# Value rows in groups of 64 columns, a 512 + 128 split of the last output tile, and its last store on ScalarE's queue

## The chip, the cores and the metric

The kernel runs on one core of one Trainium2 chip. Its engines are TensorE (PE in the profile; PEld is its weight load), VectorE (DVE), ScalarE (ACT), GpSimd (POOL) and SyncE (SP). Each has its own instruction queue and they meet through semaphores. DMA transfers are issued here from SyncE and ScalarE. The metric is the device time of one execution in microseconds (us), lower is better; three executions of the kernel before gave 269.50, 269.57 and 269.68, median 269.57.

## The reference

One layer norm feeds two branches whose results are added to the input: linear attention with a learned feature map (32 heads of 20 columns), and a gated MLP. S = 2048 rows, D = 640, F = 1536, all in bf16.

```python
xn = layernorm(x)
q, k, v = split(xn @ wqkv)                       # 32 heads, 20 columns each
pq, pk = q @ w_phi, k @ w_phi                    # per head
phi = lambda p: concat(softmax(p), softmax(-p))  # 40 features
kv  = einsum("bhsf,bhsd->bhfd", phi(pk), v)      # summed over all rows
z   = einsum("bhsf->bhf", phi(pk))
o   = (phi(pq) @ kv) / (phi(pq) . z + 1e-6)
h   = silu(xn @ w1) * (xn @ w3)
out = x + o @ wo + h @ w2
```

## The kernel before

The 2048 rows are T = 16 tiles of 128 rows. w_phi is folded into the query and key weights (Wqp, Wkp) on TensorE, so one product gives the features. Each piece of work is a generator in a list of streams (L768 to L910). A planner (L915 to L956) builds the next step of each stream, sums costs written into the source for every engine, and commits the step that can start first; ties go by the list. So the order on every engine follows from these costs, and an edit that changes a cost or a dependency can move steps. `_Program` finds dependencies by memory: an operation's accesses are cut into granules of GRAN bytes (L67 to L95), and two operations that touch one granule are ordered (L120 to L152). PSUM counts by whole banks. The source line of all instructions but DMAs is therefore L102, and of DMAs L114; the profile tells them apart by tiles.

What the change touches, in order of time:

- **Warm-up** (`warm_up`, `idle`, L506 to L513): TensorE multiplies zeros into PSUM bank 7 while the first rows of x load, 7 times 512 columns and 11 times 128.
- **Norms** (`ln_half`, `ln_rstd`, L453 to L471): statistics in `bst`, mean and variance in `mv`, scale in `rstd`, a row of each for every tile (L290 to L292).
- **Values** (`v_part`, `v_tile`, `v_store`, L556 to L566): 10 matmuls of 320 columns put a tile's values into two PSUM banks, columns 0 to 319 of each. ScalarE copies them to `v2`, where a head takes 21 columns, 20 values and a one. The ones are written once by a GpSimd memset (L450), between the norms.
- **Keys** (`k_tile`, `k_norm`, L568 to L582): ScalarE writes exp of both signs to `ekt`; VectorE sums it, and GpSimd scales it in two halves of 640 columns a tile.
- **Key-value sum** (`kv_sum`, L590 to L596): for every tile 11 matmuls, one for each group of three heads (the last has two). The weights are 128 columns of `ekt` from column 120·g, the moving operand is `v2` from column 21·h, 63 columns wide (42 in the last group). It runs in four parts of four tiles (L837 to L854). `kv_store` masks the sum and puts it to `KVc`, in groups of 64 columns; its unused columns are cleared by a memset on GpSimd.
- **Query product** (`q_tok`, L660 to L672): 11 matmuls of 63 columns a tile, weights `eqT`, moving operand `KVc` from column 64·g. They write the same PSUM columns as the sum (`at_group`).
- **Output** (`out_tile`, L693 to L712): 17 weight tiles (5 of oT, 12 of hT) by 640 columns in two halves of 320, one add of the input on VectorE, one store. The last tile is done in 384 and then 256 columns, each with its own add and store from SyncE.

`v2` shares its memory with `oT`; the arena of 212,832 bytes for a partition is full.

Of the kernel before, what the change touches and what calls it, by code (L numbers as in the profile page):

```python
# [3 lines left out]
ACT = mybir.ActivationFunctionType  # L4
# [5 lines left out]
D = 640  # L10
H = 32
DH = 20
F = 1536
T = S // 128
DC = D // 128
FC = F // 128
NB = S // 512
NG = 11
# [1 line left out]
DEN_EPS = 1e-6  # L20

ENGINES = ("PE", "ACT", "DVE", "POOL", "SP")
GRAN = 32


def heads_of_chunk(c):
# [17 lines left out]
class _Program:  # L44
# [22 lines left out]
    def regions(self, ap):  # L67
# [25 lines left out]
        for r in runs:  # L93
            g.update(range((b + r * esz) // GRAN, (b + (r + length) * esz - 1) // GRAN + 1))
        return list(g)  # L95
# [154 lines left out]
def bass_parallel_sum__linear_kernel_hedgehog__glu_gated_swiglu__prompt_kernel(  # L250
# [11 lines left out]
    bf = DT.bfloat16  # L262
    LAG = 4.0
    QLEAD = 2
    IDLE1, IDLE2 = 11, 8
    f32 = DT.float32
    P = _Program(nc)

# [5 lines left out]
    def region(size):  # L274
        o = top[0]
        top[0] = o + (size + 31) // 32 * 32
        assert top[0] <= arena_size, top[0]
        return a0 + o

    def new(name, shape, dtype, offset=None):  # L280
        size = mybir.dt.size(dtype)
        for n in shape[1:]:
            size *= n
        return P.sbuf(name, shape, dtype, region(size) if offset is None else offset)
# [2 lines left out]
    GM = new("GM", [128, DC, H], bf)  # L287
    phi_s = new("phi_s", [128, DC, DH], bf)
    BDc = new("BDc", [128, DC, 8 * DH], bf)
    bst = new("bst", [128, T, 16], f32)  # L290
    mv = new("mv", [128, T, 8], f32)
    rstd = new("rstd", [128, T, 8], f32)  # L292
    mhalf = new("mhalf", [128, 4], f32)
    warm = new("warm", [128, 8], f32)
    M3 = new("M3", [128, 4], bf)
# [2 lines left out]
    xnT = new("xnT", [128, DC, S], bf)  # L298
# [14 lines left out]
    wv = new("wv", [128, DC, D], bf, RKV + 6400)  # L313
# [6 lines left out]
    ekt = new("ekt", [128, T * 2 * D + 48], bf, RE)  # L320
# [3 lines left out]
    eqT = [new(f"eqT{i}", [128, NG, 128], bf, (RKV, RE + 27648)[i // 2] + 5632 + 2816 * (i % 2)) for i in range(4)]  # L324
    hT = [hT0, hT1, hT2, hT3]

    RV = region(21504)
    v2 = new("v2", [128, T, H * 21], bf, RV)
    oT = new("oT", [128, DC, S], bf, RV)

    RW = region(12800)
# [8 lines left out]
    PS = nc.alloc_psum_tensor("PS", [128, 8 * 512], f32)  # L340
# [3 lines left out]
    def bank(k, cols=512, off=0, rows=128):  # L344
        return PS[0:rows, k * 512 + off:k * 512 + off + cols]

    def bank2(k, cols):
        return PS[:, k * 512:(k + 2) * 512].rearrange("p (b c) -> p b c", c=512)[:, :, 0:cols]


    def mm(o, l, r, start, stop, shared=False, cost=None):
        n = free(r)
        P.op("PE", "matmul", [o], [l, r], (o, l, r),
             dict(start=start, stop=stop, skip_group_check=shared),
             cost=max(n / 2400 + 0.003, 0.055) if cost is None else cost)
# [5 lines left out]
    def free(ap):  # L361
        n = 1
        for s in ap.shape[1:]:
            n *= s
        return n

    def act(o, i, f, scale=1.0):
        P.op("ACT", "activation", [o], [i], (o, i, f), dict(scale=scale),
             cost=0.17 + free(o) / 1200)

    def tt(eng, o, a, b, f, fast=1):
        c = 0.16 + free(o) / 960 / fast if eng == "DVE" else 0.2 + free(o) * 1.7 / 1000
        P.op(eng, "tensor_tensor", [o], [a, b], (o, a, b, f), cost=c)
# [17 lines left out]
    def memset(eng, o, v):  # L391
        P.op(eng, "memset", [o], [], (o, v), cost=0.15 + free(o) / 960)

    def select(o, base, pattern, cm, cmp, fill):
        P.op("POOL", "affine_select", [o], [o], (),
             dict(out=o, in_=o, compare_op=cmp, fill=fill, base=base, pattern=pattern,
                  channel_multiplier=cm), cost=0.3 + free(o) / 960)
# [3 lines left out]
    out_t = out.rearrange("b (t p) d -> p (b t) d", p=128)  # L401
# [43 lines left out]
    def consts_late():  # L445
        memset("POOL", M3[:, 0:3], 1.0)
        select(M3[:, 0:3], 0, [[-40, 3]], 1, ALU.is_ge, 0.0)
        select(M3[:, 0:3], 40, [[40, 3]], -1, ALU.is_gt, 0.0)
        memset("POOL", ekt[:, T * 2 * D:T * 2 * D + 48], 1.0)
        memset("POOL", v2[:].rearrange("p t (h c) -> p t h c", c=21)[:, :, :, DH], 1.0)  # L450


    def ln_half(t, q):  # L453
        i, o = x_tok[:, t, 320 * q:320 * q + 320], bst[:, t, 6 * q:6 * q + 6]
        P.op("DVE", "bn_stats", [o], [i], (o, i), cost=0.48)
# [48 lines left out]
                 cost=0.9)  # L504

    def warm_up():  # L506
        idle(7, 512)
        idle(IDLE1, 128)

    def idle(n, cols):  # L510
        z = t1[:, 2, :]
        for _ in range(n):
            mm(bank(7, cols), z[:, 0:128], z[:, 0:cols], True, True, cost=cols / 1200)  # L513

    def xn_transpose(t, k):
        dst = xnT[:, :, t * 128:(t + 1) * 128]
# [30 lines left out]
        evac(dst[:, dc, :].rearrange("p (b c) -> p b c", c=320), bank2(k, 320))  # L547


    def proj(t, w, k):  # L550
        for q in range(2):
            for i in range(DC):
                mm(bank(k + q, 320), xnT[:, i, t * 128:(t + 1) * 128],
                   w[:, i, 320 * q:320 * q + 320], i == 0, i == DC - 1)

    def v_part(t, q, i, k):  # L556
        mm(bank(k + q, 320), xnT[:, i, t * 128:(t + 1) * 128], wv[:, i, 320 * q:320 * q + 320],
           i == 0, i == DC - 1)

    def v_store(t, k):  # L560
        pv = bank2(k, 320).rearrange("p b (h c) -> p b h c", c=DH)
        act(v2[:, t, :].rearrange("p (b h c) -> p b h c", b=2, c=21)[:, :, :, 0:DH], pv, ACT.Copy)

    def v_tile(t, k):
        proj(t, wv, k)
        v_store(t, k)  # L566

    def k_tile(t, k):  # L568
# [15 lines left out]
    def group(g):  # L584
        return 3 * g, min(3, H - 3 * g)

    def at_group(k, g, n):
        return bank(k + g // 8, n, 64 * (g % 8))

    def kv_sum(t0, t1, k):  # L590
        for t in range(t0, t1):
            for g in range(NG):
                h, nh = group(g)
                w = t * 2 * D + 120 * g
                mm(at_group(k, g, 21 * nh), ekt[:, w:w + 128], v2[:, t, 21 * h:21 * (h + nh)],
                   t == 0 and g % 8 == 0, t == T - 1 and g in (7, NG - 1), True, 0.03)  # L596

    def kv_store(k):
# [89 lines left out]
    finish = []  # L688

    def load_xres(t):  # L690
        P.dma("SP", xres[:, t % 4, :], x_t[:, t, :])

    def out_tile(t, k):  # L693
        b, ti = divmod(t, 4)
        if t + 2 < T:
            load_xres(t + 2)
        chunks = [(oT[:, i, t * 128:(t + 1) * 128], wo_s, i) for i in range(DC)]
        chunks += [(hT[b][:, i, ti * 128:(ti + 1) * 128], w2_s, i) for i in range(FC)]
        if t == T - 1:
            for q, lo, hi in ((0, 0, 384), (1, 384, D)):  # L700
                for n, (l, w, i) in enumerate(chunks):
                    mm(bank(k + q, hi - lo), l, w[:, i, lo:hi], n == 0, n == len(chunks) - 1)
                r = xres[:, t % 4, lo:hi]
                tt("DVE", r, bank(k + q, hi - lo), r, ALU.add)
                finish.append(P.dma("SP", out_t[:, t, lo:hi], r))
            return
        for n, (l, w, i) in enumerate(chunks):
            for q in range(2):
                mm(bank(k + q, 320), l, w[:, i, 320 * q:320 * q + 320], n == 0, n == len(chunks) - 1)
        r = xres[:, t % 4, :].rearrange("p (b c) -> p b c", c=320)  # L710
        tt("DVE", r, bank2(k, 320), r, ALU.add)
        finish.append(P.dma("SP", out_t[:, t, :], xres[:, t % 4, :]))  # L712
# [4 lines left out]
    def banks(n):  # L717

        def free_at(k):
            return max([o.end for i in range(k, k + n) for o in P.bank.get(("P", i), {}).values()],  # L720
                       default=0.0)
        return min((k for k in range(0, 8, n) if k // 2 not in held), key=free_at)
# [85 lines left out]
    def attention():  # L808
        def v(t):
            return lambda: v_tile(t, banks(2))  # L810

        yield warm_up
        for t in range(4):
            while done["t"] <= t:
                yield None
            k = banks(2)
            held.add(k // 2)
            for q in range(2):
                for i in range(DC):
                    yield lambda t=t, q=q, i=i, k=k: v_part(t, q, i, k)  # L820
            yield lambda t=t, k=k: v_store(t, k)
            held.clear()
        while done["f"] < 1:
            yield None
        for t in range(T):
            while done["t"] <= t:
                yield None
            yield lambda t=t: k_tile(t, banks(2))
            done["k"] = t + 1
            if t >= 4:  # L830
                yield v(t)
            if 9 <= t < 14:
                yield lambda dc=t - 9: fold_mm(0, dc, banks(2))
        yield lambda: P.dma("SP", wo_s[:], A_wo.rearrange("(c p) d -> p c d", p=128))
        done["v"] = 1
# [81 lines left out]
    n = len(streams)  # L917
    heads, alive = [None] * n, [True] * n
    while any(alive):
# [32 lines left out]
        i, ops, after = best[2:]  # L952
# [65 lines left out]
```

## Time and profile before

| | us |
|---|---|
| median of 3 runs (lowest to highest) | 269.57 (269.50 to 269.68) |
| the profiled execution | 269.42 |
| its span | 267.7 |
| TensorE busy, with 1943 matmul records | 262.3 |
| VectorE / GpSimd / ScalarE busy | 171.3 / 103.0 / 99.5 |

The span runs from the first to the last instruction that the profiler saw; 1.7 us of the execution lie outside it. A row of a group view names engine, operation, output tile, input tiles, shapes and count, then the busy time, the mean of one in ns, and the idle time of the engine just before such instructions with what ended it. In a timeline row stand start, length (from the first start to the last end of a merged run), engine and operation. Matmuls overlap in the pipeline, and the end of one is modelled, so the time of a step is best read from start to start. A few matmul records are missing in the trace (1943 of 1962).

How the load lies over the span, in 40 slices of 6.7 us, in tenths:

```profile
PE   7999999999999999999999999999999999999996
DVE  4559899998886878888888887898512121212112
ACT  5557979988324443334442344322100000000000
POOL 4316748999996364444444444420000000000000
PEclk9999999999999999999999999999999999999999
```

The first two slices hold the norms and the loads; up to the tenth slice come values and keys beside the first MLP steps; then the key-value sum; then queries, their products and the rest of the MLP; from about 190 us the output product alone, with VectorE adding.

### The profile page before, as it was taken

What the parts mean: (1) busy time and instruction counts of PE and PEld (TensorE: products, weight loads), DVE (VectorE), ACT (ScalarE), POOL (GpSimd) and SP (SyncE); (2) the same over time, 40 slices, a digit from 0 to 9 for tenths busy, and PEclk for the clock granted to TensorE, in tenths of its full rate; (3) what the DMA queues carried; (4) which work ended last, traced back from release to release, by engine and by line L of the source; (5) the groups of instructions that cost most, each with busy time, mean ns of one, the idle gap of its engine ahead of it and who ended that gap; (6) DMA issues with size and microseconds to landing.
All of it is one profiled execution on the core that took longest, in us unless ns stands there. A gap on an engine that the chain in (4) does not pass through costs nothing.

```text
span 267.7 us, 4797 instructions
## 1 busy us (share of the span) xinstructions
PE 262.3 (98%) x1943; PEld 160.9 (60%) x1962; DVE 171.3 (64%) x292; ACT 99.5 (37%) x193; POOL 103.0 (38%) x144
## 2 busy tenths in 40 slices
PE   7999999999999999999999999999999999999996
PEld 4656677776745545554455455444577777777774
DVE  4559899998886878888888887898512121212112
ACT  5557979988324443334442344322100000000000
POOL 4316748999996364444444444420000000000000
PEclk9999999999999999999999999999999999999999
DMA  7998695900093444555474464214212213131301
GB/s 223 279 322 155 148 220 109 309 12 2 2 326 73 78 78 81 97 100 95 78 88 95 78 82 78 44 38 78 49 51 74 75 55 94 51 98 49 95 30 49
DMA packets 63510, 27.73 MB, mean 104 GB/s; under 512 B 49792, under 2 KB 63488, under 8 KB 63488
## 3 DMA queue, kind: packets, MB, share of 16 engines
q1 hardware_dynamic: 62688, 26.94, 43.4%
q10 hardware_dynamic: 800, 0.49, 0.6%
q8 instruction: 15, 0.25, 0.4%
q14 instruction: 7, 0.06, 0.1%
HBM read 12.81 MB, written 2.62 MB: 58 GB/s over the span
## 4 chain that ended last, share of the span: by engine, by line
PE 96%; DMA 1%; ACT 1%; issue 1%; DVE 0%; POOL 0%; SPq 0%
PE PS L102 96%; DMA x_tok<-in_A_x_dram 1%; ACT t L102 1%; POOL rstd L102 0%; DVE x_tok L102 0%; DVE xres L102 0%; SPq L114 0%; DVE rstd L102 0%; DVE mv L102 0%
## 5 line engine op out<-in xcount | busy, mean ns | idle before, releaser
L102 PE MATMUL PS<-xnT,w_s 128*128 128x512 bf16 x464 | 105.7, 379 | 1.0 <-ACT Wkp L102 0.2
L102 PEld LDWEIGHTS PS<-xnT,w_s 128*128 128x128 bf16 x480 | 45.8, 98 | 51.3 <-ACT Wkp L102 0.2
L102 PE MATMUL PS<-w_s,hT 128*128 128x320 bf16 (+2 forms) x384 | 54.9, 299 | 0.0
L102 DVE TENSOR_TENSOR xres<-PS,xres 128x640 bf16<-128x640 f32 (+2 forms) x17 | 13.4, 785 | 60.0 <-PE PS L102 60.0
L102 ACT ACTIVATE th<-PS 128x512 f32<-128x512 f32 x48 | 28.8, 600 | 49.0 <-PE PS L102 49.0
L102 PEld LDWEIGHTS PS<-w_s,hT 128*128 128x128 bf16 x384 | 37.6, 98 | 14.6
L102 DVE SCALAR_TENSOR_TENSOR t<-th,PS 128x512 bf16<-128x512 f32 x48 | 32.4, 675 | 20.8 <-ACT th L102 20.8
L102 POOL TENSOR_TENSOR ekt<-ekt,rS 128x640 bf16<-128x640 bf16 x32 | 39.5, 1277 | 0.6 <-DVE rS L102 0.6
L102 ACT ACTIVATE eq<-PS 128x600 bf16<-128x600 f32 (+1 forms) x72 | 24.7, 411 | 29.6 <-PE PS L102 29.5
L102 DVE SCALAR_TENSOR_TENSOR hT<-t,PS 128x512 bf16<-128x512 bf16 x48 | 33.0, 687 | 1.7
L102 PE MATMUL PS<-wv,xnT 128*128 128x320 bf16 x160 | 24.7, 299 | 0.1
L102 PE MATMUL PS<-wo_s,oT 128*128 128x320 bf16 (+2 forms) x160 | 24.5, 299 | 0.0
L102 PE MATMUL PS<-Wkp,xnT 128*128 128x320 bf16 x160 | 23.9, 299 | 0.0
L102 ACT ACTIVATE ekt<-PS 128x640 bf16<-128x640 f32 x32 | 22.3, 703 | 3.8 <-PE PS L102 3.3
L102 PE MATMUL PS<-Wqp,xnT 128*128 128x128 bf16 (+1 forms) x157 | 23.5, 297 | 0.2
L102 POOL TENSOR_TENSOR eq<-eq,rq 128x600 bf16<-128x600 bf16 (+1 forms) x32 | 22.6, 728 | 1.3
L102 DVE TENSOR_REDUCE S<-ekt 128x64 f32<-128x1280 bf16 x16 | 23.0, 1438 | 0.0
L102 POOL TENSOR_TENSOR rq<-rq,Sq 128x32 f32<-128x32 f32 x16 | 4.0, 253 | 48.5 <-DVE rq L102 48.5
L102 POOL TENSOR_TENSOR half<-eq 128x660 f32<-128x660 bf16 x15 | 20.4, 1359 | 3.6 <-ACT eq L102 3.6
L102 PEld LDWEIGHTS PS<-wo_s,oT 128*128 128x128 bf16 x160 | 15.7, 98 | 6.3
L102 PEld LDWEIGHTS PS<-wv,xnT 128*128 128x128 bf16 x160 | 15.3, 98 | 6.5 <-ACT xnT L102 0.5
L102 PEld LDWEIGHTS PS<-Wqp,xnT 128*128 128x128 bf16 x160 | 12.9, 98 | 10.5
(56 smaller groups left out, 182.7 us busy)
## 6 DMA issues: line engine op xcount, KB each, us to landing
w_s<-in_B_w_dram SPq DMA_DIRECT2D x6, 640.0 KB, 6.2
xres<-in_A_x_dram SPq DMA_DIRECT2D x16, 160.0 KB, 2.4
out_dram<-xres SPq DMA_DIRECT2D x15, 160.0 KB, 1.8
x_tok<-in_A_x_dram SPq DMA_DIRECT2D x3, 640.0 KB, 6.4
w_s<-in_B_w_dram SPq DMA_DIRECT2D x1, 1920.0 KB, 8.0
wo_s<-in_A_wo_dram SPq DMA_DIRECT2D x1, 800.0 KB, 8.5
x_tok<-in_A_x_dram SPq DMA_DIRECT2D x3, 160.0 KB, 4.1
wv<-in_A_wqkv_dram ACTq DMA_DIRECT2D x1, 400.0 KB, 4.3
```

Source lines behind the costliest of these rows:

```text
L102: o = _Op(eng, lambda: m(*args, **kw), r, w, cost)
```

## The change

- GRAN goes from 32 to 8 bytes.
- The rows of `bst`, `mv` and `rstd` shrink from 16, 8 and 8 words to 12, 2 and 2 (1024 bytes less for a partition).
- `v2` gets 64 columns for a group of three heads instead of 63, 704 for a tile instead of 672 (1024 bytes more). The ones and the key-value sum's moving operand follow.
- The values' PSUM halves stand in columns 192 to 511 of one bank and 0 to 319 of the next, so that a tile's 640 values are one row of PSUM. ScalarE reads 660 columns from there, 33 heads of 20; the last 20 lie behind the values, and go to columns of `v2` that the sum doesn't read.
- The 512-column warm-up matmuls are 8 and go to banks 7 down to 0; the 128-column ones are 7.
- The last output tile is cut into 512 and 128 columns, and the second store is issued by ScalarE.

In the built program the warm-up's counts change, the last of the four parts of the key-value sum stands one MLP step earlier on TensorE (30 instead of 40 MLP matmuls behind the third part), and from there to about the end of the queries some query, product and MLP steps change places. On GpSimd the clearing of `KVc` stands ahead of the first query scaling. SyncE loses the last store, which ScalarE gets.

```diff
-GRAN = 32
+GRAN = 8
...
-    IDLE1, IDLE2 = 11, 8
+    IDLE1, IDLE2 = 7, 8
...
-    bst = new("bst", [128, T, 16], f32)
-    mv = new("mv", [128, T, 8], f32)
-    rstd = new("rstd", [128, T, 8], f32)
+    bst = new("bst", [128, T, 12], f32)
+    mv = new("mv", [128, T, 2], f32)
+    rstd = new("rstd", [128, T, 2], f32)
...
-    RV = region(21504)
-    v2 = new("v2", [128, T, H * 21], bf, RV)
+    RV = region(T * NG * 128)
+    v2 = new("v2", [128, T, NG * 64], bf, RV)
...
-        memset("POOL", v2[:].rearrange("p t (h c) -> p t h c", c=21)[:, :, :, DH], 1.0)
+        memset("POOL", v_heads(v2[:].rearrange("p t n -> p (t n)"))[:, :, :, DH], 1.0)
+
+    def v_heads(a):
+        return a.rearrange("p (g x) -> p g x", x=64)[:, :, 0:63].rearrange("p g (h c) -> p g h c", c=21)
...
-        idle(7, 512)
+        idle(8, 512)
         idle(IDLE1, 128)
...
-        for _ in range(n):
-            mm(bank(7, cols), z[:, 0:128], z[:, 0:cols], True, True, cost=cols / 1200)
+        for i in range(n):
+            j = 7 - i if cols == 512 else 7
+            mm(bank(j, cols), z[:, 0:128], z[:, 0:cols], True, True, cost=cols / 1200)
...
+    def part(w, t, q, i, k, off=0):
+        mm(bank(k + q, 320, 0 if q else off), xnT[:, i, t * 128:(t + 1) * 128], w[:, i, 320 * q:320 * q + 320],
+           i == 0, i == DC - 1)
...
     def v_store(t, k):
-        pv = bank2(k, 320).rearrange("p b (h c) -> p b h c", c=DH)
-        act(v2[:, t, :].rearrange("p (b h c) -> p b h c", b=2, c=21)[:, :, :, 0:DH], pv, ACT.Copy)
+        pv = PS[:, k * 512 + 192:k * 512 + 192 + 60 * NG].rearrange("p (g h c) -> p g h c", h=3, c=DH)
+        act(v_heads(v2[:, t, :])[:, :, :, 0:DH], pv, ACT.Copy)
 
     def v_tile(t, k):
-        proj(t, wv, k)
+        proj(t, wv, k, 192)
         v_store(t, k)
...
-                h, nh = group(g)
+                nh = group(g)[1]
                 w = t * 2 * D + 120 * g
-                mm(at_group(k, g, 21 * nh), ekt[:, w:w + 128], v2[:, t, 21 * h:21 * (h + nh)],
+                mm(at_group(k, g, 21 * nh), ekt[:, w:w + 128], v2[:, t, 64 * g:64 * g + 21 * nh],
...
-            for q, lo, hi in ((0, 0, 384), (1, 384, D)):
+            for q, lo, hi in ((0, 0, 512), (1, 512, D)):
...
-                finish.append(P.dma("SP", out_t[:, t, lo:hi], r))
+                finish.append(P.dma(("SP", "ACT")[q], out_t[:, t, lo:hi], r))
...
-                    yield lambda t=t, q=q, i=i, k=k: v_part(t, q, i, k)
+                    yield lambda t=t, q=q, i=i, k=k: part(wv, t, q, i, k, 192)
```

More of the change, by code (lines that the diff above doesn't have):

```diff
@@ L547, in fold_mm, with proj @@
         evac(dst[:, dc, :].rearrange("p (b c) -> p b c", c=320), bank2(k, 320))
-    def proj(t, w, k):
+    def part(w, t, q, i, k, off=0):
+        mm(bank(k + q, 320, 0 if q else off), xnT[:, i, t * 128:(t + 1) * 128], w[:, i, 320 * q:320 * q + 320],
+           i == 0, i == DC - 1)
+    def proj(t, w, k, off=0):
         for q in range(2):
             for i in range(DC):
[L553 to L558, printed above, removed]
+                part(w, t, q, i, k, off)
     def v_store(t, k):
-        pv = bank2(k, 320).rearrange("p b (h c) -> p b h c", c=DH)
-        act(v2[:, t, :].rearrange("p (b h c) -> p b h c", b=2, c=21)[:, :, :, 0:DH], pv, ACT.Copy)
+        pv = PS[:, k * 512 + 192:k * 512 + 192 + 60 * NG].rearrange("p (g h c) -> p g h c", h=3, c=DH)
+        act(v_heads(v2[:, t, :])[:, :, :, 0:DH], pv, ACT.Copy)
     def v_tile(t, k):
-        proj(t, wv, k)
+        proj(t, wv, k, 192)
         v_store(t, k)
```

## The prediction

> **What bounds the kernel now.** I read the page's first table, then the chain of waits, then the list of waits, then the timeline of single stretches.
>
> ```profile
> span 267.7 us, 4797 instructions
> PE 262.3 (98%) x1943; PEld 160.9 (60%) x1962; DVE 171.3 (64%) x292; ACT 99.5 (37%) x193; POOL 103.0 (38%) x144
> PE 96%; DMA 1%; ACT 1%; issue 1%; DVE 0%; POOL 0%; SPq 0%
> ```
>
> TensorE is busy in 98% of the span and holds 96% of the chain that ends last; no other engine passes 64%. What is left for the others is at the two ends, as the pieces of that chain in order of time show:
>
> ```profile
> 1.26 2.69 DMA x_tok<-in_A_x_dram
> ...
> 7.31 5.00 PE PS L102 x43
> ...
> 19.91 0.23 issue
> 20.14 7.54 PE PS L102 x49
> ...
> 183.47 81.73 PE PS L102 x589
> ...
> 265.23 0.42 DVE xres L102
> ```
>
> At 7.31 us the chain passes to TensorE and stays there to 265.2 us; the last gap that is worth a name lies at 19.91. After 265.2 come one add on VectorE and the last store, 2.5 us in all to the end of the span at 267.7. So the time changes in three ways only: TensorE's own steps get shorter or longer, TensorE is made to wait, or the tail after its last matmul changes. The list of waits has little to give back in TensorE's own rows:
>
> ```profile
> PE PS L102 <- DVE warm L102: 1.3, 1, 1.3
> PE PS L102 <- DVE x_tok L102: 0.3, 2, 0.2
> PE PS L102 <- ACT Wkp L102: 0.2, 1, 0.2
> ```
>
> The third is the gap at 19.91, and the others lie ahead of it. The change leaves the order of every engine there as it was, warm-up aside.
>
> **Value groups of 64 columns: the steps of the key-value sum.** The sum issues 176 matmuls (16 tiles of 11 groups). Before, group g of a tile starts 126·g bytes into the row; after, 128·g. The rows below are the busy time of instructions that touch the values in the two stretches where the sum runs, then the same for the products with KVc, which have the same 11 steps of 63 columns and the same PSUM places, but read groups of 64 columns already (columns: stretch, length, TensorE busy and count, weight loads and others).
>
> ```profile
> 68.72:72.81 4.09, 4.09 (x132) 4.09 (x131) 0.00 (x0) 0.00 (x0) 1.00 0.01 4
> 81.45:82.81 1.36, 1.36 (x44) 1.36 (x43) 0.00 (x0) 0.00 (x0) 1.00 0.21 43
> 87.68:88.00 0.32, 0.32 (x11) 1.00 0.00 0
> 66.56 2.32 PE L102 MATMUL PS<-xnT,w_s 128*128 128x512 bf16 x10
> 68.72 4.25 PE L102 MATMUL PS<-v,ekt 128*128 128x63 bf16 x132
> ```
>
> Now: (4.09 + 1.36) / 176 = 31.0 ns a step. With KVc: 0.32 / 11 = 29.1 ns. If the difference comes from where the moving operand starts, 16 tiles at 0.32 take 5.12 instead of 5.45: **0.33 us saved**. Bounds: nothing, if it comes from the weights (key exponentials at 240-byte steps, which do not change); and, from the other side, 63 columns can't go faster than a 512-column stream, whose ten steps take 68.72 − 66.56 = 2.16, 216 ns each or 2.37 columns a ns, so 26.6 ns a step and 0.77 us saved. I take 0.33, since the KVc row is the nearest in every respect. TensorE is alone on the path here, so it all counts.
>
> The Trainium skill's page "TensorE: Matmul & The Clock Gate", section "Back-to-back issue gap", gives a warm step as columns / 2.4 + 2.5 ns, 28.75 ns at 63, with no term for an address. The KVc steps agree (29.1), the value steps do not (31.0); taken literally, the rule would leave the values' excess to another cause and the time at the third rival's.
>
> **The stores of the values.** They run on ScalarE and grow from 640 to 660 columns (20 of junk beside head 31, which no sum reads).
>
> ```profile
> L102 ACT ACTIVATE v<-PS 128x640 bf16<-128x640 f32 x16 | 11.2, 701 | 2.4 <-PE PS L102 2.3
> L102 ACT ACTIVATE ekt<-PS 128x640 bf16<-128x640 f32 x32 | 22.3, 703 | 3.8 <-PE PS L102 3.3
> L102 ACT ACTIVATE eq<-PS 128x600 bf16<-128x600 f32 x32 | 21.4, 669 | 25.0 <-PE PS L102 25.0
> ```
>
> (703 − 669) / 40 = 0.85 ns a column, so 17 ns each. ScalarE itself waits for TensorE in these groups and TensorE never for a value store, so 16 × 17 ns costs nothing; without cover it would be 0.27 us.
>
> **The ones in the values' 21st columns.** One GpSimd memset goes from 512 elements with one step to 528 elements in 176 rows of 3. GpSimd then normalizes key tiles almost without a break, and the last part of the key-value sum waits for the last of them. That part is also put one MLP step (10 matmuls) earlier in the changed program's order: 30 instead of 40 stand ahead of it.
>
> ```profile
> 25.64 2.37 POOL L102 MEMSET v<- 128x512 bf16 x1
> 78.31 1.27 POOL L102 TENSOR_TENSOR ekt<-ekt,rS 128x640 bf16<-128x640 bf16 x1
> L102 POOL TENSOR_TENSOR ekt<-ekt,rS 128x640 bf16<-128x640 bf16 x32 | 39.5, 1277 | 0.6 <-DVE rS L102 0.6
> L102 POOL TENSOR_TENSOR half<-eq 128x660 f32<-128x660 bf16 x15 | 20.4, 1359 | 3.6 <-ACT eq L102 3.6
> L102 POOL TENSOR_TENSOR eq<-eq,rq 128x600 bf16<-128x600 bf16 x16 | 19.2, 1203 | 1.3
> ```
>
> The last part would start at 81.45 − 2.16 − 132 × 0.0019 = 79.04. Tile 15 comes 33 steps later, and its sixth group is the first that needs the last normalization: 79.04 + 38 × 0.029 = 80.14. That one ends at 78.31 + 1.27 = 79.58. Cover: **0.56 us**. The memset's price: 2.37 / 512 = 4.6 ns an element gives 2.44; for rows, 30 rows of 20 take 1203 and 32 rows 1277, 37 ns for 20 elements, so `half` (66 rows of 10) has 1359 − 1277 − 37 = 45 ns for 34 more rows, 1.3 ns each, 0.23 us for 176. That is 2.67, 0.30 later, inside the cover: **0**. From below it could be quicker by a little, which nobody waits for; from above, each short row at the price of a row of 20 (1277 / 32 = 40 ns) gives 7.0 us, a stall of 4.6 − 0.56 = 4.1 us. I take the memset's own row, and keep the far end as a rival.
>
> Moving the part earlier changes no work: the MLP step that stood ahead of it stands behind it. Between it and the first product with KVc now lie 10 query and 30 MLP matmuls instead of 20 and 10. On GpSimd the small KVc memset now stands ahead of the first query scaling, which delays that tile's transposing DMA by its 0.15 us; in the changed order that product comes later than before, not sooner. SyncE's order is unchanged up to the last store. What queues behind a late normalization is in-order TensorE, and behind it ScalarE and VectorE, so a stall there would be paid in full.
>
> **Norm buffers, finer bookkeeping.** Smaller rows make room for the wider values. The norms of the start keep order and instructions: 0. The granularity of 8 bytes removes waits at most; after 21 us TensorE has none to lose.
>
> **Warm-up.** 7 × 512 + 11 × 128 columns become 8 × 512 + 7 × 128: 4992 both times.
>
> ```profile
> 3.36 0.15 PEld L102 LDWEIGHTS PS<-t 128*128 128x128 bf16 x1 [0.28 <-issue]
> 3.79 0.15 PEld L102 LDWEIGHTS PS<-t 128*128 128x128 bf16 x1 [0.28 <-issue]
> 4.21 1.11 PEld L102 LDWEIGHTS PS<-t 128*128 128x128 bf16 x10 [0.28 <-issue]
> 5.79 0.45 PE L102 MATMUL PS<-ident,x_tok 128*128 128x128 bf16 x5 [0.20 <-DVE x_tok L102]
> ```
>
> A wide one takes 0.43, four narrow ones 4 × 0.107 = 0.43, so the warm-up ends at the same moment, ahead of the transposes at 5.79 that wait for VectorE anyway: 0.
>
> **The tail.** The last tile goes from 384 + 256 columns to 512 + 128, and the 128-column store to ScalarE's queue.
>
> ```profile
> 87.40 0.44 PE L102 MATMUL PS<-Wqp,xnT 128*128 128x128 bf16 x5
> 87.68 0.48 PE L102 MATMUL PS<-KVc,eqT 128*128 128x63 bf16 x11
> 260.41 0.98 PE L102 MATMUL PS<-wo_s,oT 128*128 128x384 bf16 x5
> 263.17 0.71 PE L102 MATMUL PS<-wo_s,oT 128*128 128x256 bf16 x5
> 263.37 0.56 DVE L102 TENSOR_TENSOR xres<-PS,xres 128x384 bf16<-128x384 f32 x1 [1.94 <-PE PS L102]
> 263.72 1.47 PE L102 MATMUL PS<-w_s,hT 128*128 128x256 bf16 x12
> 265.23 0.42 DVE L102 TENSOR_TENSOR xres<-PS,xres 128x256 bf16<-128x256 f32 x1 [1.30 <-PE PS L102]
> x_tok<-in_A_x_dram ACTq DMA_DIRECT2D x1, 80.0 KB, 2.5
> x_tok<-in_A_x_dram SPq DMA_DIRECT2D x1, 80.0 KB, 2.3
> out_dram<-xres SPq DMA_DIRECT2D x1, 96.0 KB, 1.6
> out_dram<-xres SPq DMA_DIRECT2D x1, 64.0 KB, 1.5
> ```
>
> TensorE: before, 263.17 − 260.41 = 2.76 for 17 steps of 384, and 17 × (263.72 − 263.17) / 5 = 1.87 for 256, together 4.63. After, 17 × 0.216 + 17 × 0.056 (87.68 − 87.40 over 5) = 4.62: no difference. The add: 0.56 − 0.42 for 128 columns, so 0.13 off the last one. The first add (0.69) runs from about 264.3 to 265.0, before the last can start at 265.2; without those 0.2 us it would push the last add. The store: 32 KB less took 0.1 less (1.6 to 1.5), so 1.4 on SyncE's queue. ScalarE's queue never stored; its one like transfer landed 0.2 later than SyncE's, both issued together on the same engines, so 0 to 0.2 more; I take 0.05, as these shared. Tail: 0.13 + 0.10 − 0.05 = **0.18 us saved**, from 0.03 to 0.23.
>
> The Trainium skill's "DMA: Bandwidth & Descriptors", "Specifications", wants at least 512 bytes for line rate and says that smaller writes are read and rewritten; the new store has rows of 256. By it the last store would not shrink below 1.5 and the tail would give 0.08; no row here has a store of such rows.
>
> **Sum.** 0.33 + 0.18 = 0.51. The profiled execution took 269.42, 1.7 outside its span, and would take 268.91; the median of the runs stands 0.15 above it, so 269.57 − 0.51 = **269.06**. What this kernel's measurement can tell from no change is about 0.2%, 0.54 us, so the forecast lies at that bound.
>
> **Rivals.** *Steps at the column rate* (0.16): aligned steps drop below 29.1, towards 26.6, as the KVc steps may carry a cost of their own. 0.77 + 0.18 gives 268.62 at the end. For it: one group in eleven has 42 columns. Against: no row has 63 columns that fast.
>
> *A late memset* (0.16, slower): short rows make it long, GpSimd has no pause to catch up in, and the moved part of the sum meets it. Beyond 0.56 + 0.51 = 1.07 us more (3.44 in all) the kernel is slower than before; at twice its time, 4.74, the stall is 2.37 − 0.56 = 1.81 and the time 269.57 − 0.51 + 1.81 = 270.87. For it: 0.6 us of idle time before the normalizations. Against: 1.3 ns a row.
>
> *Weights, not values* (0.06): the 31.0 ns come from the weights, and only the tail is left: 269.39. The page's rule above has no address term either.
>
> **How the numbers follow.** The forecast has 0.62, its own range 268.85 to 269.3; the bound of 0.2% (269.03) halves it: 0.30 below, 0.32 within. Faster 0.30 + 0.16 = 0.46; same 0.32 + 0.06 = 0.38; slower 0.16. The range runs from the fast rival's end to just past the third's: 268.6 to 269.55; it leaves out the slow rival.
>
> **What would show it.** The stretch of the key-value sum: 176 steps in 5.1 us; 5.45 means that the weights set it. The memset: below 2.9 us, and no wait of TensorE for GpSimd between 79 and 81 us. The tail: last add 0.29 us, last landing 1.4 to 1.6 after its issue. Any TensorE wait between 21 and 265 us, or a start that passes to TensorE later, would make the prediction wrong.

## The result and the profile after

| | before | after |
|---|---|---|
| median of 12 runs each, side by side (lowest to highest), us | 269.51 (269.32 to 269.81) | 268.88 (268.84 to 269.00) |
| ratio of after to before, 95% interval | | 0.9977 (0.9970 to 0.9985) |
| the profiled execution / its span, us | 269.42 / 267.7 | 268.84 / 267.1 |
| key-value sum: 176 steps, us | 5.45 | 5.07 |
| last add / last store, issue to landing, us | 0.42 / 1.54 | 0.29 / 1.49 |
| memset of the ones, us | 2.37 | 2.46 |

The changed kernel is 0.63 us faster, a little more than the 0.54 us (0.2% of the time) that the prediction took as the least that can be told from no change. One run each of tail_only and big_buffers below, 277.92 and 346.28 us, stood far above its fellows and is left out of the ratios. The landing of one store is read from the trace's semaphore events, one place finer than the list of transfers gives it.

The first table of the changed kernel's page:

```profile
span 267.1 us, 4814 instructions
PE 263.3 (99%) x1959; PEld 159.7 (60%) x1959; DVE 170.0 (64%) x292; ACT 98.0 (37%) x193; POOL 102.9 (39%) x144
```

TensorE's busy time looks 1.0 us longer in a span that is 0.6 shorter. That is a matter of records: this trace has all 1959 matmuls, that of before 1943 of 1962, and a lost record is lost busy time. For such a difference one reads from start to start instead. The pieces of the chain in order of time:

```profile
7.29 5.00 PE PS L102 x43
...
19.89 0.01 issue
19.89 244.91 PE PS L102 x1826
264.80 0.02 issue
264.82 0.29 DVE xres L102
```

The chain passes to TensorE at 7.29 (7.31 before) and TensorE keeps it to the last add, which starts at 264.82 instead of 265.23. So TensorE is done 0.41 us earlier: 0.02 is the earlier start, and 0.39 went out of its own work. The start is no gain of the change: in the traces of the other runs TensorE takes over the chain between 7.20 (memset_twice) and 7.46 us (tail_only). The gap of 0.23 at 19.91 in the chain of before has no counterpart here. It was not a saving: nothing before the key-value sum moved, which starts at 68.70 against 68.72. The only row of the list of waits in which a matmul waits for another engine stands ahead of the first transposes:

```profile
PE PS L102 <- DVE warm L102: 1.3, 1, 1.3
```

The 0.39 are found in the key-value sum. These are the busy times of instructions that touch the values, in stretches cut from the first step to the start of what follows the last:

```profile
68.70:72.50 3.80, 3.80 (x132) 3.80 (x131) 0.00 (x0) 0.00 (x0) 1.00 0.02 4
78.97:80.24 1.27, 1.26 (x44) 1.26 (x43) 0.00 (x0) 0.00 (x0) 1.00 1.06 357
sum 5.07, PE 5.06 PEld 5.06 ACT 0.00 POOL 0.00; mean PE 2.53 PEld 2.53 ACT 0.00 POOL 0.00
```

The same view of the products with KVc, in one stretch of 11 steps:

```profile
88.07:88.39 0.32, 0.31 (x11) 1.00 0.00 0
```

5.07 / 176 is 28.8 ns a step, against 31.0 before. Now the sum runs at about the pace of the products with KVc, which did not change: within their 16 tiles the trace has 29.08 ns from start to start on the mean, in both kernels. The last part starts at 78.97 instead of 81.45, as the one MLP step that stood ahead of it now stands behind.

The tail, in the timeline of the changed kernel (start, length, engine, operation; the bracket is the idle time ahead and what ended it):

```profile
260.00 1.24 PE L102 MATMUL PS<-wo_s,oT 128*128 128x512 bf16 x5
...
263.67 0.44 PE L102 MATMUL PS<-wo_s,oT 128*128 128x128 bf16 x5
263.87 0.69 DVE L102 TENSOR_TENSOR xres<-PS,xres 128x512 bf16<-128x512 f32 x1 [2.84 <-PE PS L102]
263.95 0.83 PE L102 MATMUL PS<-w_s,hT 128*128 128x128 bf16 x12
264.82 0.29 DVE L102 TENSOR_TENSOR xres<-PS,xres 128x128 bf16<-128x128 f32 x1 [0.26 <-PE PS L102]
265.14 0.36 ACTq L114 DMA_DIRECT2D out_dram<-xres  x1
```

From the last tile's first matmul to the start of its last add it takes 264.82 − 260.00 = 4.82, and 265.23 − 260.41 = 4.82 before: the other cut costs TensorE nothing. The first add ends at 264.56, 0.26 ahead of the last one's start. What is left of the tail is the shorter add (0.42 to 0.29) and the landing (1.54 to 1.49). Start 0.02, steps 0.385, add 0.135 and landing 0.05 make 0.59, the difference of the two spans.

### The profile page after: what moved, and what is told of

It is laid out like the page before. It is cut to its first block, busy times and chain, and to the rows that moved or that the text cites. A ratio compares the mean times of both kernels' runs of the same rounds, so it can differ in the third digit from the quotient of the medians.

```text
span 267.1 us, 4814 instructions
## 1 busy us (share of the span) xinstructions
PE 263.3 (99%) x1959; PEld 159.7 (60%) x1959; DVE 170.0 (64%) x292; ACT 98.0 (37%) x193; POOL 102.9 (39%) x144
## 4 chain that ended last, share of the span: by engine, by line
PE 96%; DMA 1%; ACT 1%; DVE 0%; POOL 0%; issue 0%; SPq 0%
PE PS L102 96%; DMA x_tok<-in_A_x_dram 1%; ACT t L102 1%; POOL rstd L102 0%; DVE x_tok L102 0%; SPq L114 0%; DVE xres L102 0%; DVE rstd L102 0%; DVE mv L102 0%
## 5 line engine op out<-in xcount | busy, mean ns | idle before, releaser
L102 PE MATMUL PS<-xnT,w_s 128*128 128x512 bf16 x480 | 107.7, 379 | 0.0
L102 ACT ACTIVATE eq<-PS 128x600 bf16<-128x600 f32 (+1 forms) x72 | 23.8, 424 | 29.7 <-PE PS L102 29.7
L102 PE MATMUL PS<-Wqp,xnT 128*128 128x512 bf16 (+1 forms) x160 | 24.2, 299 | 0.0
L102 ACT ACTIVATE ekt<-PS 128x640 bf16<-128x640 f32 x32 | 20.6, 708 | 4.8 <-PE PS L102 4.8
```

Source lines behind the costliest of these rows:

```text
L102: o = _Op(eng, lambda: m(*args, **kw), r, w, cost)
```

## The experiments

**The two halves of the change, one at a time.** *kv_only* is the changed kernel with the old tail, so it has the granules, the small rows and the warm-up of the change as well as the wide values; *tail_only* is the kernel before with the new tail. Each ran in five rounds on one chip beside the kernel before, whose median there was 269.51 in 30 runs.

```diff
 # kv_only, against the changed kernel
-            for q, lo, hi in ((0, 0, 512), (1, 512, D)):
+            for q, lo, hi in ((0, 0, 384), (1, 384, D)):
...
-                finish.append(P.dma(("SP", "ACT")[q], out_t[:, t, lo:hi], r))
+                finish.append(P.dma("SP", out_t[:, t, lo:hi], r))
```

```diff
 # tail_only, against the kernel before
-            for q, lo, hi in ((0, 0, 384), (1, 384, D)):
+            for q, lo, hi in ((0, 0, 512), (1, 512, D)):
...
-                finish.append(P.dma("SP", out_t[:, t, lo:hi], r))
+                finish.append(P.dma(("SP", "ACT")[q], out_t[:, t, lo:hi], r))
```

> The changed kernel with the old tail (384 + 256 columns, both stores on SyncE). Theory (the gain is 0.39 us of shorter key-value steps plus 0.19 us of a shorter tail): about 269.07, 0.4 under the kernel before; the 176 steps of the sum in 5.07 us, last add 0.425 us, last landing 1.54 us after its issue. Rival (the whole gain is in the steps and the order on TensorE, the tail gives nothing): 268.9. Rival (the whole gain is the tail): 269.5.

> The kernel before with the new tail alone. Theory: 0.19 us under the kernel before, about 269.3; the steps of the sum still in 5.45 us; last add 0.29 us, last landing 1.49 us after its issue on ScalarE's queue. Rival (a store of 256-byte rows or a first store from ScalarE eats what the add saves): no difference, 269.5.

kv_only took 269.07 us, ratio 0.9983 (0.9974 to 0.9992). tail_only took 269.33, ratio 0.9991 (0.9982 to 1.0); its interval touches 1, so by the clock alone its gain is not certain. The profiles show where each gain lies. The last rows of the value view, first of kv_only, then of tail_only:

```profile
sum 5.06, PE 5.06 PEld 5.06 ACT 0.00 POOL 0.00; mean PE 2.53 PEld 2.53 ACT 0.00 POOL 0.00
```

```profile
sum 5.46, PE 5.46 PEld 5.45 ACT 0.00 POOL 0.00; mean PE 2.73 PEld 2.73 ACT 0.00 POOL 0.00
```

The short steps come without the new tail, and the new tail does not bring them; that they belong to the values' rows is tried further down. Tail_only's timeline has the tail of the changed kernel, 0.55 later: 0.39 of that are the longer steps, and the sum started 0.17 later in that execution (68.87 against 68.70).

```profile
265.37 0.29 DVE L102 TENSOR_TENSOR xres<-PS,xres 128x128 bf16<-128x128 f32 x1 [0.26 <-PE PS L102]
265.70 0.36 ACTq L114 DMA_DIRECT2D out_dram<-xres  x1
```

By the medians the halves give 0.44 and 0.18, and 0.62 together, where the whole change gives 0.63: they add up. The intervals are wide beside that, about 0.25 us either way each. The other parts of the change are in kv_only, whose shorter steps alone account for 0.385 of its 0.44, so no gain of theirs can be told.

**The queue of the last store.** *tail_sp* is the changed kernel with that store back on SyncE.

```diff
-                finish.append(P.dma(("SP", "ACT")[q], out_t[:, t, lo:hi], r))
+                finish.append(P.dma("SP", out_t[:, t, lo:hi], r))
```

> The changed kernel with its last store of 128 columns back on SyncE's queue. Theory (stores shrink by about 0.1 us for 32 KB on SyncE, and ScalarE's queue costs some of it): landing 1.43 us after the issue instead of 1.49, time 0.05 lower, 268.83, hardly to be told from 268.88. Rival (256-byte rows are rewritten, so the store cannot shrink): landing 1.5, no difference. Rival (SyncE is held by its list of waits or by the first store's issue): landing or issue later, 269.0 or more.

268.85 us, ratio 0.9975 (0.9965 to 0.9985). The list of transfers, first of tail_sp, then of the changed kernel (queue, count, size, median us from issue to landing):

```profile
out_dram<-xres SPq DMA_DIRECT2D x1, 32.0 KB, 1.5
```

```profile
out_dram<-xres ACTq DMA_DIRECT2D x1, 32.0 KB, 1.5
```

In the events the store lands after 1.47 us on SyncE's queue and 1.49 on ScalarE's, so moving it costs about 0.02 us and gains nothing that can be measured. SyncE's queue also prices the size: 1.54 for the 64 KB of before, 1.47 for 32 KB, 0.07 less. The Trainium skill's "DMA: Bandwidth & Descriptors", "Specifications", says that writes below 512 bytes are read and rewritten; a store of 256-byte rows still landed sooner than one of 512-byte rows here, if by less than the 0.10 that was forecast.

**The norm buffers and the finer granules.** *big_buffers* is the changed kernel with the old rows and granules.

```diff
-GRAN = 8
+GRAN = 32
...
-    bst = new("bst", [128, T, 12], f32)
-    mv = new("mv", [128, T, 2], f32)
-    rstd = new("rstd", [128, T, 2], f32)
+    bst = new("bst", [128, T, 16], f32)
+    mv = new("mv", [128, T, 8], f32)
+    rstd = new("rstd", [128, T, 8], f32)
```

> The changed kernel with the old norm buffers and the old granularity of 32 bytes. It has the order of the kernel before on every engine, so the last part of the key-value sum stands behind 40 MLP matmuls again. Theory (the order is neutral, since TensorE never waits): the same time as the changed kernel, 268.88, no TensorE wait after 21 us, steps of the sum in 5.07 us. Rival (the finer granularity and the moved steps gave part of the gain): 269.0 to 269.4.

268.93 us, ratio 0.9978 (0.9969 to 0.9987): the same time. Two things changed inside it. The last part of the key-value sum stands behind 40 MLP matmuls again and starts at 81.16, so it was the granules or the rows that moved it in the planner, and its place costs nothing. And VectorE's norm statistics run slower, as in the kernel before. The group and the timeline row from the norms' stretch, of the changed kernel and then of big_buffers:

```profile
L102 DVE BATCH_NORM_STATS2 bst<-x_tok 128x6 f32<-128x320 bf16 x24 | 9.9, 475 | 0.0
```

```profile
19.10 1.66 DVE L102 BATCH_NORM_STATS2 bst<-x_tok 128x6 f32<-128x320 bf16 x4
```

```profile
L102 DVE BATCH_NORM_STATS2 bst<-x_tok 128x6 f32<-128x320 bf16 x24 | 11.2, 486 | 0.4
```

```profile
19.13 1.94 DVE L102 BATCH_NORM_STATS2 bst<-x_tok 128x6 f32<-128x320 bf16 x4
```

Four statistics take 1.66 us with the change and 1.94 without, 0.28 less. A tile's two halves write 24 bytes each into one row of `bst`; in granules of 32 bytes both touch the first one, and the second is ordered behind the first, in granules of 8 they share none. The traces show that order: in big_buffers the second statistic of a tile waits for VectorE's own semaphore and starts 35 ns after the first has ended, in the changed kernel it has no such wait and starts about 80 ns before that end. That the granules took the wait away, and not the smaller rows, is argued from the addresses; the two were not tried apart. Six such groups are 1.7 us; 0.25 of it goes into a longer wait of VectorE for GpSimd's `rstd` (1.08 against 0.83). GpSimd, which waits for their results, starts its long run of key normalizations earlier, as the timelines of the changed kernel and of big_buffers show:

```profile
25.07 2.46 POOL L102 MEMSET v<- 128x528 bf16 x1
...
41.36 36.91 POOL L102 TENSOR_TENSOR ekt<-ekt,rS 128x640 bf16<-128x640 bf16 x30 [0.60 <-DVE rS L102]
```

```profile
25.66 2.46 POOL L102 MEMSET v<- 128x528 bf16 x1
...
42.77 36.95 POOL L102 TENSOR_TENSOR ekt<-ekt,rS 128x640 bf16<-128x640 bf16 x30 [0.59 <-DVE rS L102]
```

1.41 us earlier on GpSimd, and nothing in the time, as TensorE waits for neither.

**What makes a step short.** The values differ from before in two ways: their rows are wider, and each group now starts at a multiple of 128 bytes instead of 126. The shift runs keep the width and move all the values by a few bytes. The Trainium skill's "SBUF — State Buffer", "Specifications (TRN2)", gives cache lines of 16 bytes and a penalty for each crossing into a new one; 126 bytes touch 8 such lines from an offset of 0 or 2, and 9 from 4 to 14 (the last group's 84 bytes touch 6, and 7 from 14). In the kernel before, group g starts at 126·g bytes, and only the groups 0 and 8 start at a multiple of 16.

```diff
 # shift_2; in shift_4, shift_8, shift_14 and shift_16 column 2, 4, 7 and 8 in place of 1
...
-    RV = region(T * NG * 128)
-    v2 = new("v2", [128, T, NG * 64], bf, RV)
+    RV = region(T * NG * 128 + 32)
+    v2f = new("v2", [128, T * NG * 64 + 16], bf, RV)
+    v2 = v2f[:, 1:1 + T * NG * 64].rearrange("p (t n) -> p t n", t=T)
...
```

> The changed kernel with all value groups moved by 2 bytes, so that no moving operand of the sum starts at a multiple of 16 bytes; the order and all else stay. Theory (the operand's start sets the step): all ten 63-column steps of a tile at 32 ns, 176 steps in about 5.55 us, 0.48 more than the changed kernel. Rival (the weights set it, or the PSUM place, or the group's row of 126 bytes crossing lines): 5.07 as in the changed kernel.

> The same, moved by 8 bytes. Theory with a granule of 16 bytes: 5.55 us for the 176 steps. With a granule of 8 bytes or less: 5.07.

> The same, moved by 16 bytes. Theory with a granule of 16 bytes: 5.07 us for the 176 steps. With a granule of 32 bytes or more: 5.55.

After these three had shown that an offset of 2 costs little, two more were to tell a count of lines from an odd start:

> The changed kernel with all value groups moved by 4 bytes. A row of 126 bytes then ends 2 bytes past a multiple of 128 and touches nine 16-byte lines, as it does when moved by 8; moved by 2 it touched eight, took 5.20 us and not the 5.55 that the theory had. Theory (the count of 16-byte lines sets the step, with a small toll for any odd start): 5.49 us for the 176 steps. Rival (the distance of the start from the line sets it, a little more for every 2 bytes): about 5.3.

> The same, moved by 14 bytes: nine lines again. Count of lines: 5.49 us for the 176 steps. Distance of the start, growing with the bytes past the line: 5.5 or more; shrinking again towards the next line: about 5.2.

One execution each (the kernel before took 269.72 beside the offsets of 2, 8 and 16, and 269.46 beside 4 and 14):

| offset in bytes | lines of 16 bytes for 126 bytes | 176 steps, us | ns a step | time, us |
|---|---|---|---|---|
| 0 (the changed kernel) | 8 | 5.07 | 28.8 | 268.88 (median) |
| 2 | 8 | 5.21 | 29.6 | 268.91 |
| 4 | 9 | 5.46 | 31.0 | 269.17 |
| 8 | 9 | 5.50 | 31.3 | 269.31 |
| 14 | 9 | 5.54 | 31.5 | 269.32 |
| 16 | 8 | 5.07 | 28.8 | 268.77 |

The last row of the value view, of shift_2, shift_4, shift_8 and shift_14:

```profile
sum 5.21, PE 5.20 PEld 5.20 ACT 0.00 POOL 0.00; mean PE 2.60 PEld 2.60 ACT 0.00 POOL 0.00
```

```profile
sum 5.46, PE 5.46 PEld 5.45 ACT 0.00 POOL 0.00; mean PE 2.73 PEld 2.73 ACT 0.00 POOL 0.00
```

```profile
sum 5.50, PE 5.49 PEld 5.49 ACT 0.00 POOL 0.00; mean PE 2.75 PEld 2.75 ACT 0.00 POOL 0.00
```

```profile
sum 5.54, PE 5.53 PEld 5.53 ACT 0.00 POOL 0.00; mean PE 2.77 PEld 2.76 ACT 0.00 POOL 0.00
```

The weights are the same in all of them, and the order of the work on every engine too, so the weights are out. It is not the wider rows either, as shift_8 has them and steps as slowly as the kernel before. The expectation that any offset but a multiple of 16 costs the whole 0.4 us failed at 2 bytes, where a third of it is lost. On the mean of a tile's eleven groups a ninth line costs 2.2 to 2.7 ns a step, an odd start within eight lines 0.8. So the count of lines fits most of it, which agrees in kind with the rule of the Trainium skill's page; that gives no price. Two things it does not give. From 4 to 14 bytes the steps still grow by 0.08 us, and 5.54 at 14 also fits the rival of a toll that grows with the distance; it is shift_4 that speaks against this rival, with 5.46 where it had 5.3. And one thing stays open: in the kernel before, group 7 starts 2 bytes behind a multiple of 16 and touches eight lines, yet its steps take 31.9 ns from start to start (mean of 16 tiles) like its neighbours' 31.5 to 32.9, while those of group 8, at a multiple of 16, take 28.1. A count of lines does not explain that.

**A late memset.** *memset_twice* writes the ones twice, which doubles the memset.

```diff
         memset("POOL", v_heads(v2[:].rearrange("p t n -> p (t n)"))[:, :, :, DH], 1.0)
+        memset("POOL", v_heads(v2[:].rearrange("p t n -> p (t n)"))[:, :, :, DH], 1.0)
```

> The changed kernel with the memset of the ones issued twice, so that GpSimd is 2.46 us later from 27.5 us on. Theory of the slow rival (no pause to catch up in, and the moved last part of the sum meets the late normalization): the last normalization ends at 78.27 + 2.46 = 80.73 instead of 78.27, tile 15's sixth group, due at about 80.1, waits about 0.65 us, time 269.5. Rival (GpSimd's idle 2.1, 1.5 and 0.45 us before its normalizations take it up): the last normalization ends at about 78.3, no wait of TensorE, 268.9.

269.64 us, 0.76 more than the changed kernel's median, but not from the place that was expected. The last key normalization ended at 80.68 as foreseen, and no step of the key-value sum waited for it. The chain of waits of memset_twice, in pieces:

```profile
27.48 2.45 POOL v L102
...
31.66 2.68 DVE x_tok L102 x2
...
36.08 0.65 DVE t L102
...
40.84 0.20 POOL rstd L102
41.07 0.92 ACT x_tok L102
41.99 0.61 ACT v L102
42.65 222.94 PE PS L102 x1676
```

Here TensorE lost the time at 36 to 43 us. The norms' scale (`rstd`) is computed on GpSimd behind the memset. VectorE, which applies it to `x_tok` in order, waits 3.57 us for it, where in the changed kernel it waits 1.08, as the timelines show, of memset_twice and of the changed kernel:

```profile
31.66 2.68 DVE L102 TENSOR_SCALAR x_tok<-x_tok,mv,rstd 128x640 bf16<-128x640 bf16 x2 [3.57 <-POOL rstd L102]
36.08 0.63 DVE L102 SCALAR_TENSOR_TENSOR t<-th,PS 128x512 bf16<-128x512 f32 x1
36.77 1.57 PE L102 MATMUL PS<-wv,xnT 128*128 128x320 bf16 x10 [0.26 <-DVE t L102]
42.65 0.58 PE L102 MATMUL PS<-wv,xnT 128*128 128x320 bf16 x3 [0.23 <-ACT v L102]
```

```profile
29.25 2.68 DVE L102 TENSOR_SCALAR x_tok<-x_tok,mv,rstd 128x640 bf16<-128x640 bf16 x2 [1.08 <-POOL rstd L102]
```

Behind `x_tok` in VectorE's queue stands the read of an MLP product out of PSUM (`t`), and the next value matmuls wait until that has freed their bank; at 42.65 the same goes through ScalarE, where a norm's scaling stands ahead of a value store. TensorE thus starts the key-value sum at 69.50 instead of 68.70, 0.80 late. It had taken over the chain 0.09 earlier than in the changed kernel (7.20 against 7.29), so it lost 0.89 on the way, 0.43 of it at 36.77 and 0.39 at 42.65 from start to start. As TensorE was late itself, the late normalizations were in time for it.

**A delay on GpSimd behind the norms.** To try the other place, four memsets of a tile that nothing reads go to GpSimd among the key normalizations. In *pool_late_30* the planner's costs keep the last part of the sum behind 30 MLP matmuls, in *pool_late_40* it comes behind 40.

```diff
+    junk = new("junk", [128, 640], bf)
...
 # in k_norm; in pool_late_40 with cost=0.0
+        if t == 8:
+            for _ in range(4):
+                P.op("POOL", "memset", [junk[:]], [], (junk[:], 1.0), cost=-0.035)
```

> The changed kernel with four memsets of a tile that nobody reads (640 columns, about 0.6 us each) on GpSimd between its key normalizations, after the norms, and the order of all other work as in the changed kernel: 30 MLP matmuls stand ahead of the last part of the key-value sum. Theory (once the norms are done, a late normalization meets that part): the last one ends at about 80.7 instead of 78.27, tile 15 is due at about 80.0, TensorE waits 0.6 to 0.8 us, time about 269.5. Rival (there is cover beyond that): no wait, 268.9.

> The same four memsets, with 40 MLP matmuls ahead of the last part, as in the kernel before (the planner's cost of a memset is 0 instead of -0.03, which moves the step back). Theory: tile 15 is due at about 82.2, after the last normalization at 80.7: no wait, 268.9.

pool_late_30 took 270.04 us, 1.16 above the changed kernel's median; of that, 0.26 was there before the sum began (68.96 instead of 68.70). It is not the memsets' work: TensorE took over the chain at 7.45 us instead of 7.29 and was 0.26 late by 9.5, long before they start at 58.85. Its timeline:

```profile
58.85 2.69 POOL L102 MEMSET junk<- 128x640 bf16 x4
61.51 19.70 POOL L102 TENSOR_TENSOR ekt<-ekt,rS 128x640 bf16<-128x640 bf16 x16
79.23 1.26 PE L102 MATMUL PS<-v,ekt 128*128 128x63 bf16 x38
81.26 0.34 PE L102 MATMUL PS<-v,ekt 128*128 128x63 bf16 x6 [0.77 <-POOL ekt L102]
```

38 steps run, and the sixth group of tile 15 waits for GpSimd, which ends its last normalization at 81.21: the place that the prediction named. The part takes 81.60 − 79.23 = 2.37 us, where an undisturbed one takes 1.43, so the stall is 0.94, more than the 0.6 to 0.8 that was expected. In pool_late_40 the same memsets cost nothing, 268.89 us, as the part starts later:

```profile
81.18 1.43 PE L102 MATMUL PS<-v,ekt 128*128 128x63 bf16 x44
```

## Why the prediction was right, point by point

- **TensorE alone sets the end**: held. The difference lies in its steps, in the tail and in a start that is 0.02 earlier.
- **The key-value sum**, forecast 0.33 from the KVc row, with 5.12 us for 176 steps: measured 5.07, 0.385 saved. The mechanism was right, and the term was 0.055 too small. The prediction took the sum's steps and the KVc steps as the same 11 of 63 columns, but the sum's last group has only 42. From start to start the sum's groups 0 to 4, which follow that narrow one, take 28.3 to 28.5 ns (means over the 16 tiles) and the others 29.0 to 29.4, while the KVc steps have 29.08; 176 × (29.08 − 28.82) is 0.045 of the 0.055. That fits the narrow group as the cause, which no run tries alone. The fast rival had named it, but its 26.6 ns a step fell, and so did the third rival, the weights. The rule quoted there, 28.75 ns a step and no term for an address, holds for the aligned steps and fails for the others (29.6 to 31.5).
- **The stores of the values**: cost nothing, as forecast. They take 719 ns instead of 701, 18 more where 17 was forecast, and no matmul waits for one in the changed kernel.
- **The memset**: forecast 2.67 us, measured 2.46, which is 2.37 / 512 × 528 = 2.44 and no toll for its rows of three, where the forecast had 0.23 from `half` (whose 34 more rows are 33, which makes it 0.24). The cost of 0 stood. The cover did not: forecast 0.56 us, measured 78.97 + 38 × 0.0288 = 80.06 less the end of the last normalization, 41.36 + 36.91 = 78.27, that is 1.8: the last normalization ends 1.31 sooner than the forecast's 79.58. Pool_late_30 agrees with it: 2.69 of filler less 1.8 is 0.9, and the part lost 0.94.
- **Norm buffers and granules**: the cost of 0 held, but "the norms of the start keep order and instructions" missed that the finer granules, or the smaller rows, let VectorE's statistics run closer. That is what widened the cover above. Nor did the smaller rows "make room" for the wider values: big_buffers holds both the old rows and the wide values, so the arena, which the description of the kernel calls full, was not: its regions add up to 211,232 of the 212,832 bytes, and the 1,024 for the values fit without the smaller rows.
- **The late memset as the slow rival**: it did not come about, but as a mechanism it is real, with the wrong place. A memset that is longer by 2.5 us meets the norms first, through VectorE's and ScalarE's queues, and the sum not at all. The threshold of 1.07 us was worked out from a place that a delay ahead of the norms does not reach; for a delay behind them, pool_late_30 shows that place and a wait there.
- **The moved part of the sum**: neutral in itself, as forecast (big_buffers). It did give up cover: the same late GpSimd costs 0.94 us behind 30 MLP matmuls and nothing behind 40.
- **Warm-up**: 0, as forecast: the transposes' chain starts at 7.29 against 7.31.
- **The tail**: forecast 0.13 + 0.10 − 0.05, measured 0.135 + 0.07 − 0.02, the same 0.18 within 0.01, and tail_only gives 0.18 by the medians.
- **The sum**: 0.51 forecast, 0.59 between the spans, 0.63 between the medians. The time came out 0.18 below the forecast: 0.06 is the kernel before, with a median of 269.51 beside this run instead of 269.57; 0.055 the steps; 0.02 the start; the other 0.045 is not accounted for and lies within the scatter of the medians. The forecast gave this side of its bound of 0.54 us and the other nearly even chances, and the time passed it by 0.09 us, so on which side it fell was decided by terms of that size, the start and the scatter among them: that is luck, and the mechanism is not.

## What to carry to other kernels

A matmul with a narrow moving operand pays for where that operand starts: padding groups of 63 bf16 columns to 64 took 7% off the mean step here, and a small neighbour in the same profile that was already aligned gave the price in advance. When an engine ahead of the bound is made later, follow every queue that its result passes, in order of time: the first reader that stands in an in-order queue ahead of the bound's own buffers decides, not the last. Cover changes with the rest of a change: work out both ends of it in the changed order, the early engine's as well.

## What the runs showed of the hardware

- The step of 63 bf16 columns depends on the moving operand's first byte: with all groups alike, 28.8 ns from a multiple of 16, 29.6 from 2 behind it, 31.0 to 31.5 from 4 to 14 behind it (means over eleven groups, the last of 42 columns). In the kernel before, with mixed starts, the group at 2 took 31.9.
- Two statistics on VectorE that the program orders one behind the other take 0.14 us more a pair than two that it doesn't (1.94 against 1.66 for two pairs), though they run on one engine in order: the second starts 35 ns behind the first's end instead of about 80 ns ahead of it.
- The last store's landing hardly follows its size: 1.54 us for 64 KB and 1.47 for 32 KB on SyncE's queue, and 1.49 for 32 KB on ScalarE's.
- A GpSimd memset of single bf16 elements 42 bytes apart costs 4.6 to 4.7 ns each (2.37 us for 512 with one step, 2.46 for 528 in rows of three), 640 contiguous columns 0.67 us (2.69 for four), about 1 ns each.
